# Last-key scores of each head moved into the head's own half of the array

## The chip, the cores and the metric

The kernel runs on one core of one Trainium2 chip. The core has five engines with instruction queues of their own: TensorE (PE, with its weight loads shown as PEld), VectorE (DVE), ScalarE (ACT), GpSimd (POOL) and SyncE (SP). In this kernel SP issues nearly all transfers. Each engine takes its instructions in the order of the program and waits on semaphores. The metric is the device time of one execution in microseconds (us). Before the change it was 1731.4, 1735.86 and 1735.88 us in three runs, median 1735.86.

## The reference

Attention that keeps only the 32 largest scores of each query, followed by a two-layer perceptron with an exact Gelu:

```python
# q, k, v: (8, 8, 576, 64): batch, heads, sequence, head dimension
scores = scale * np.matmul(q, k.transpose(0, 1, 3, 2))
kth = np.partition(scores, -32, axis=-1)[..., -32:-31]
scores = np.where(scores >= kth, scores, -1000000000.0)
scores = scores - np.max(scores, axis=-1, keepdims=True)
attn = np.exp(scores)
attn = attn / (np.sum(attn, axis=-1, keepdims=True) + 1e-09)
x = np.matmul(attn, v)            # then (B,H,S,D) -> (4608, 512)
h = x @ w_in                      # (512, 2048)
g = 0.5 * h * (1.0 + erf(h / sqrt(2)))
return g @ w_out                  # (2048, 512)
```

## The kernel before

Two heads make a pair: the head dimension is 64, so a pair fills the 128 rows of the array, head e in rows 64e to 64e+63. The sequence of 576 is four tiles of 128 queries and a tail of 64. An item of work is one tile of 128 queries for one pair (128 such items), or the tail queries of two pairs (16 items), 144 in all. All products are f32, and an f32 product is carried out as two passes over the array, each with its own weight load: the profile counts passes.

Per item, `scores(i)` makes the scores of 128 queries against 576 keys for both heads, `top_k(i)` finds the 32nd largest value by four rounds of eight maxima on VectorE (lines 324 and 327), `softmax` is four activations on ACT (363, 364), `normalise` is on POOL (375), `transposes` turns the probabilities over on TensorE (392, 409) with copies on ACT, and `attend` multiplies by v (440, 450). The two products of the perceptron (489 and 525) are cut into pieces, and `mlp` puts seven or eight pieces into each step, between the other work of TensorE.

`scores`, the function of the change, uses two tiles of PSUM for an item. `s_ps` has two banks, one for each head, and takes the scores of the 512 main keys; there is one buffer of it. `t_ps` is one bank out of the two of the tag "tp", which transposes, attend's outputs and transpose_qk share, and takes the scores of the 64 last keys of both heads. In `qk`, which `transpose_qk` makes for each pair, columns 0 to 639 are queries, columns 640 to 767 the last keys (block diagonal: head 0's 64 keys in rows 0 to 63 and columns 640 to 703, head 1's in the rest, zeros elsewhere), and columns 768 to 1279 the main keys. Because of those zeros one product over all 128 rows gives the tails of both heads (line 281). The main keys are four products over 64 rows, 256 keys each, in the order head 0, head 1, head 0, head 1 (line 285). Two activations of ACT then scale and evict `s_ps` (289) and `t_ps` (290) to SBUF.

The order is written out by hand and nothing is rescheduled. In step n of the main loop TensorE is given scores of item n+2, attend of n-3, pieces of the perceptron, transposes of n-2 and, at set steps, the transposes of q and k of a coming pair (transpose_qk, line 249). VectorE is given top_k of item n. ACT's order in the step is the eviction of the scores, the copy of attend's output, half or all of the softmax of n-1, the copies of the transposes, Gelus and copies of y as the pieces come up, and in the first steps the conversion of the weights. SP's queue holds, in the same order, the loads of q and k for the pair after next (eight issues of lines 94 and 97, put there by the last piece of transpose_qk), the loads of v (four issues for each pair), the loads of the weights (lines 152 and 161, in the first 17 steps, each waiting for VectorE's or POOL's last use of its staging buffer), and the stores of the output (line 514, each waiting for the ACT copy of y at line 531). No instruction of the score products stands on SP.

Of the kernel before, what the change touches and what calls it, by code (L numbers as in the profile page):

```python
# [14 lines left out]
def kernel(  # L15
# [19 lines left out]
    nc = tc.nc  # L35
# [5 lines left out]
    B, H, S, D = q.shape  # L41
    P = 128
# [5 lines left out]
    SM = NM * P  # L48
    TL = S - SM
# [185 lines left out]
    KT = SM + 2 * P  # L235
# [31 lines left out]
    def spread(t, step, n):  # L267

        return bass.AP(tensor=t.tensor, offset=t.offset, ap=[list(t.ap[0]), [step, 2], [1, n]])

    def scores(i):
        if i >= N:
            return
        pair, t = items[i]
        S_of[i] = s = work.tile([P, 2 * S], f32, tag="s", bufs=5, name="s")
        s_ps = ps.tile([P, 2, 512], f32, tag="s", bufs=1, name="s_ps")
        t_ps = ps.tile([P, 512], f32, tag="tp", name="t_ps")
        if t < NM:
            qk = qk_of[pair]
            lhsT = qk[:, t * P : (t + 1) * P]  # L280
            nc.tensor.matmul(t_ps[:, 0:P], lhsT=lhsT, rhs=qk[:, SM + P : KT], start=True, stop=True)  # L281
            for c in range(2):
                for e in range(2):
                    rows = slice(e * D, (e + 1) * D)
                    nc.tensor.matmul(  # L285
                        s_ps[:, e, c * 256 : (c + 1) * 256], lhsT=lhsT[rows, :],
                        rhs=qk[rows, KT + c * 256 : KT + (c + 1) * 256], start=True, stop=True,
                    )
            nc.scalar.activation(spread(s, S + TL, SM), s_ps, func=AF.Copy, scale=scale)  # L289
            nc.scalar.activation(s[:, SM : S + TL], t_ps[:, 0:P], func=AF.Copy, scale=scale)  # L290
        else:
            for r in range(2):
                qk = qk_of[pair + r]
                lhsT = qk[:, SM : SM + P]
                nc.tensor.matmul(s_ps[:, r, :], lhsT=lhsT, rhs=qk[:, KT:], start=True, stop=True)  # L295
                for e in range(2):
                    nc.tensor.matmul(  # L297
                        t_ps[:, r * TL : (r + 1) * TL], lhsT=lhsT,
                        rhs=qk[:, SM + P + e * TL : SM + P + (e + 1) * TL],
                        start=(e == 0), stop=(e == 1),  # L300
                    )
            s2 = s.rearrange("p (r n) -> p r n", r=2)
            nc.scalar.activation(s2[:, :, 0:SM], s_ps, func=AF.Copy, scale=scale)
            nc.scalar.activation(
                s2[:, :, SM:S], t_ps[:, 0:P].rearrange("p (r n) -> p r n", r=2),
                func=AF.Copy, scale=scale,
            )
# [270 lines left out]
    for pair in range(2):  # L578
        for piece in transpose_qk(pair, pair == 0):
            piece()  # L580
        if pair == 0:
            scores(0)
            scores(1)
# [8 lines left out]
    for n in range(ahead):  # L592

        left[0] = 7 if n < START + 2 * NP else 8
        weights_add(unit_in(n))
        scores(n + 2)
        product = attend(n - 3)
        late = n > START
# [71 lines left out]
```

## Time and profile before

| | |
|---|---|
| profiled execution | 1733.63 us |
| its span | 1731.9 us |
| mean granted TensorE clock | 0.974 |
| TensorE busy | 1632.1 us, 94% of the span |
| VectorE busy | 1428.2 us, 82% |
| ACT busy | 1191.1 us, 69% |
| POOL busy | 664.0 us, 38% |
| tail products (line 281) | 256 passes, 52.9 us |
| main score products (line 285) | 1024 passes, 153.7 us |
| SP transfers issued | 448 |

A line of the timeline gives start, length, engine, source line, operation, and out<-in with its shapes; "xN" means N instructions merged, and the brackets give the engine's idle time before it and what ended it. "SPq" is a transfer being issued on SP; its length is the time for which SP is held by the issue, not that of the transfer. The recorded end of a matmul is modelled, so that the next one can start before it. A line of the windows gives a stretch, its length, the busy time of each engine with the number of its instructions, the granted clock of TensorE and the load on DMA. Busy shares over the whole span are means over stages that have different limits.

### The profile page before, as it was taken

The numbers are of one execution on the slowest core, as the hardware profiler recorded it, in microseconds if no ns is written. First come the engines' busy times: TensorE is split into PE (matmuls) and PEld (weight loads), VectorE is DVE, ScalarE is ACT, GpSimd is POOL, SyncE is SP. The second block draws the span as 40 slices with busy tenths as digits, with TensorE's granted clock in tenths as the row PEclk, the third lists the DMA queues.
The fourth block names the chain that finished last, engine by engine and source line by source line (L and its number), as shares of the span: only waits on it lengthen the run. The fifth ranks groups of instructions, "written<-read, shape, count | busy, mean of one in ns | idle before, by whom it ended". The sixth has DMA issues, their size and how long they took to land.

```text
span 1731.9 us, 24265 instructions
## 1 busy us (share of the span) xinstructions
PE 1632.1 (94%) x8416; PEld 1115.4 (64%) x8416; DVE 1428.2 (82%) x3042; ACT 1191.1 (69%) x2147; POOL 664.0 (38%) x764
## 2 busy tenths in 40 slices
PE   5558999999999999999999999999999999999999
PEld 3335667766666667666666667676666666766665
DVE  7998888988799887997989878898889987899900
ACT  6877767777677767777767666776767766777730
POOL 3677733333333333332333323333333332333310
PEclk8679999999999999999999999999999999999999
DMA  5422310011100111002100011001110010000000
GB/s 155 132 98 91 86 41 1 13 27 28 41 7 13 28 34 34 1 17 45 28 27 1 27 41 41 1 13 27 28 47 1 13 28 14 20 1 13 7 13 13
DMA packets 126716, 56.10 MB, mean 32 GB/s; under 512 B 117889, under 2 KB 117889, under 8 KB 126593
## 3 DMA queue, kind: packets, MB, share of 16 engines
q1 hardware_dynamic: 125056, 52.16, 11.3%
q0 software_dynamic: 320, 2.10, 0.3%
q8 instruction: 67, 1.10, 0.3%
q14 instruction: 57, 0.46, 0.1%
q10 hardware_dynamic: 1216, 0.30, 0.1%
HBM read 45.08 MB, written 9.44 MB: 31 GB/s over the span
## 4 chain that ended last, share of the span: by engine, by line
PE 84%; ACT 5%; POOL 0%; issue 0%; ACTq 0%; POOLq 0%
PE y_ps L525 27%; PE h_ps L489 27%; PE o L440 8%; PE s_ps L285 7%; PE tp L409 7%; PE o L450 2%; PE t_ps L281 1%; PE s_ps L295 1%; PE tp_qk L249 1%; ACT L364 1%; ACT s L364 1%; ACT s L363 1%; PE t_ps L297 1%; PE tp_t L392 1%; POOL s L375 0%; ACT L500 0%
## 5 line engine op out<-in xcount | busy, mean ns | idle before, releaser
L324 DVE MAX8 top<-rest 128x8 f32<-128x576 f32 x864 | 610.3, 749 | 0.0
L489 PE MATMUL h_ps<-xT,w_in_sb 128*128 128x256 f32 (+1 forms) x2560 | 562.9, 364 | 4.3 <-ACT g L500 4.3
L525 PE MATMUL y_ps<-w_out_sb,g 128*128 128x512 f32 x1152 | 545.7, 598 | 0.0
L375 POOL TENSOR_SCALAR s<-s,rden 128x576 f32<-128x576 f32 x288 | 494.3, 1725 | 0.8 <-issue 0.4
L489 PEld LDWEIGHTS h_ps<-xT,w_in_sb 128*128 128x128 f32 x2560 | 432.5, 193 | 67.1 <-issue 15.8
L327 DVE MATCH_REPLACE8 rest<-top,rest 128x576 f32<-128x576 f32 x576 | 423.9, 745 | 0.0
L356 POOL TENSOR_SCALAR den<-den 128x2 f32<-128x2 f32 x144 | 32.1, 223 | 902.1 <-ACT s L364 901.2
L525 PEld LDWEIGHTS y_ps<-w_out_sb,g 128*128 128x128 f32 x1152 | 196.3, 190 | 166.9 <-issue 166.6
L289 ACT ACTIVATE s<-s_ps 128x1024 f32<-128x1024 f32 x128 | 131.6, 1028 | 188.3 <-PE s_ps L285 188.3
L364 ACT ACTIVATE s<-s,bias 128x576 f32<-128x576 f32 x288 | 223.3, 775 | 12.8
L363 ACT ACTIVATE s<-s,neg 128x576 f32<-128x576 f32 x288 | 223.7, 777 | 1.2 <-POOL neg L339 0.7
L416 ACT COPY pt<-tp 128x512 f32<-128x512 f32 x256 | 147.6, 577 | 108.3 <-PE tp L409 107.8
L409 PEld LDWEIGHTS tp<-ident,s 128*128 128x128 f32 x1152 | 148.5, 146 | 113.1 <-issue 59.8
L327 DVE MATCH_REPLACE8 rest<-top,s 128x576 f32<-128x576 f32 x288 | 211.9, 744 | 0.0
L324 DVE MAX8 top<-s 128x8 f32<-128x576 f32 x288 | 202.0, 744 | 5.1 <-ACT s L290 5.1
L409 PE MATMUL tp<-ident,s 128*128 128x128 f32 x1152 | 180.9, 283 | 23.4 <-ACT qk L253 12.8
L350 DVE RECIPROCAL rden<-den 128x2 f32<-128x2 f32 x144 | 23.4, 162 | 213.4 <-POOL den L356 213.4
L285 PE MATMUL s_ps<-qk 64*128 64x256 f32 x1024 | 153.7, 421 | 3.5 <-ACT s L289 3.5
L440 PE MATMUL o<-pt,raw_v 128*64 128x256 f32 x1280 | 153.5, 386 | 2.1 <-ACT pt L416 2.1
L440 PEld LDWEIGHTS o<-pt,raw_v 128*64 128x64 f32 x1280 | 86.8, 138 | 61.1 <-issue 16.1
L285 PEld LDWEIGHTS s_ps<-qk 64*128 64x128 f32 x1024 | 92.6, 195 | 26.8 <-ACT s L289 4.0
L500 ACT ACTIVATE g<-h_ps 128x512 f32<-128x512 f32 x144 | 78.6, 594 | 37.8 <-PE h_ps L489 37.1
(65 smaller groups left out, 1149.8 us busy)
## 6 DMA issues: line engine op xcount, KB each, us to landing
raw_q<-in_q_dram SPq DMA_DIRECT2D x64, 128.0 KB, 2.3
raw_v<-in_v_dram SPq DMA_DIRECT2D x64, 128.0 KB, 2.4
out_dram<-y SPq DMA_DIRECT2D x32, 256.0 KB, 2.2
raw_k<-in_k_dram SPq DMA_DIRECT2D x62, 128.0 KB, 2.4
w_out_sb<-in_moe_w_in_dram SPq DMA_DIRECT2D x12, 511.8 KB, 4.9
w_out_sb<-in_moe_w_out_dram SPq DMA_DIRECT2D x10, 511.8 KB, 3.9
w_out_sb<-in_moe_w_in_dram POOLq DMA_DIRECT2D x4, 511.8 KB, 7.7
words<-in_moe_w_out_dram SPq DMA_DIRECT2D x4, 511.8 KB, 5.1
```

The source lines that it names most:

```text
L285: nc.tensor.matmul(s_ps[:, e, c * 256 : (c + 1) * 256], lhsT=lhsT[rows, :], rhs=qk[rows, KT + c * 256 : KT + (c + 1) * 256], start=True, s ...
L289: nc.scalar.activation(spread(s, S + TL, SM), s_ps, func=AF.Copy, scale=scale)
L324: nc.vector.max(st["top"][:, e, 8 * r : 8 * r + 8], cur[e])
L327: nc.vector.match_replace(rest[:, e], st["top"][:, e, 8 * r : 8 * r + 8], cur[e], LOWEST)
L363: nc.scalar.activation(s, s, func=AF.Prelu, bias=st["neg"][:, e, 1:2], scale=1.0, alpha=STEEP)
L364: nc.scalar.activation(s, s, func=AF.Exp, bias=st["bias"][:, e : e + 1], scale=1.0, accum_out=st["den"][:, e : e + 1],)
L375: nc.gpsimd.tensor_scalar(s, s, st["rden"][:, e : e + 1], None, op0=ALU.mult)
L409: nc.tensor.transpose(tp[:, j * P : (j + 1) * P], s[:, first + j * P : first + (j + 1) * P], ident)
L416: nc.scalar.copy(out=dst, in_=tp.rearrange("p (j n) -> p j n", j=NM))
L440: nc.tensor.matmul(o[e * D : (e + 1) * D, 0:n], lhsT=vt[:, j, e, :], rhs=pt[:, e * NM + j if j < NM else 2 * NM, :], start=(j == 0), stop= ...
L489: nc.tensor.matmul(h_tile(u)[:, i, :], lhsT=w_in_sb[:, ko, f * P : (f + 1) * P], rhs=xT[:, ko, c0 : c0 + n], start=(ko == 0), stop=(ko == ...
L525: nc.tensor.matmul(y_of[sub], lhsT=g_of[u][:, i, sub * P : (sub + 1) * P], rhs=w_out_sb[:, f, :], start=(f == 0), stop=(f == FT - 1),)
```

## The change

The one tail product over 128 rows becomes two products over 64 rows, each with 64 columns and each in its own head's half of the array. Head 0's comes first of the six products of the item, head 1's last. Between them stand the four main products, now in the order head 1, head 0, head 1, head 0. Both tails still write the one bank `t_ps`, in separate columns, from two different halves of the array rows. To keep them apart in time a no-op is put on SP: it waits for the first tail product, and the last tail product waits for it. The evictions and the items of tail queries stay as they are. The order of all other instructions on every engine is unchanged; SP's queue has 128 no-ops more, each in the place where its item's scores stand in the program.

```diff
             lhsT = qk[:, t * P : (t + 1) * P]
-            nc.tensor.matmul(t_ps[:, 0:P], lhsT=lhsT, rhs=qk[:, SM + P : KT], start=True, stop=True)
-            for c in range(2):
-                for e in range(2):
-                    rows = slice(e * D, (e + 1) * D)
-                    nc.tensor.matmul(
-                        s_ps[:, e, c * 256 : (c + 1) * 256], lhsT=lhsT[rows, :],
-                        rhs=qk[rows, KT + c * 256 : KT + (c + 1) * 256], start=True, stop=True,
-                    )
+            tails = [
+                (e, t_ps[:, e * TL : (e + 1) * TL], SM + P + e * TL, TL) for e in range(2)
+            ]
+            mains = [
+                (e, s_ps[:, e, c * 256 : (c + 1) * 256], KT + c * 256, 256)
+                for c in range(2) for e in (1, 0)
+            ]
+            made_by = []
+            for e, dst, at, n in tails[:1] + mains + tails[1:]:
+                rows = slice(e * D, (e + 1) * D)
+                made_by.append(nc.tensor.matmul(
+                    dst, lhsT=lhsT[rows, :], rhs=qk[rows, at : at + n], start=True, stop=True
+                ))
+                if len(made_by) == 1:
+                    between = nc.sync.nop(nofuse=True)
+
+            for a, b in ((between, made_by[0]), (made_by[-1], between)):
+                tc.add_manual_dep(
+                    a.ins, b.ins.name,
+                    mybir.DependencyInfo(mybir.DependencyClass.Sync, mybir.DependencyReason.DATA),
+                    reason="two row tiles, one bank",
+                )
             nc.scalar.activation(spread(s, S + TL, SM), s_ps, func=AF.Copy, scale=scale)
             nc.scalar.activation(s[:, SM : S + TL], t_ps[:, 0:P], func=AF.Copy, scale=scale)
```

## The prediction

> **What bounds the kernel now.** I read the page first, then busy time by stage, then narrow stretches of the timeline around the score products, on TensorE and on SyncE's (SP's) queue.
>
> ```profile
> span 1731.9 us, 24265 instructions
> PE 1632.1 (94%) x8416; PEld 1115.4 (64%) x8416; DVE 1428.2 (82%) x3042; ACT 1191.1 (69%) x2147; POOL 664.0 (38%) x764
> ...
> PE 84%; ACT 5%; POOL 0%; issue 0%; ACTq 0%; POOLq 0%
> ```
>
> ```profile
> 13.90:130.00 116.10, 63.33 (x325) 43.42 (x326) 116.10 (x236) 94.19 (x154) 71.88 (x58) 0.72 0.39 115
> 130.00:240.00 110.00, 98.28 (x506) 68.13 (x505) 94.49 (x192) 78.82 (x136) 76.36 (x58) 0.97 0.24 71
> 240.00:1731.90 1491.90, 1464.19 (x7566) 999.62 (x7564) 1216.50 (x2614) 1015.03 (x1855) 511.20 (x628) 0.99 0.08 21
> ```
>
> The columns are stretch, length, then busy time of PE, PEld, DVE, ACT and POOL, granted clock, DMA. From 13.9 to 130 us VectorE is busy without a gap (116.10 of 116.10); there TensorE has room. From 240 us on TensorE is busy 1464.19 of 1491.90, so only 27.7 us of its idle time could absorb anything: a wait put on TensorE there is paid nearly in full. The sum below is made against the profiled execution, 1733.6 us; the median of the three runs is 2.2 us above it.
>
> **The products themselves.** One score tile, and then an item tail, whose pairs of 64-column products run as four passes (an f32 product is two passes):
>
> ```profile
> 436.37 1.03 PE L489 MATMUL h_ps<-xT,w_in_sb 128*128 128x256 f32 x4
> ...
> 437.24 0.38 PE L281 MATMUL t_ps<-qk 128*128 128x128 f32 x2
> ...
> 437.55 1.14 PE L285 MATMUL s_ps<-qk 64*128 64x256 f32 x8
> ...
> 438.62 2.84 PE L525 MATMUL y_ps<-w_out_sb,g 128*128 128x512 f32 x6
> ```
>
> ```profile
> 200.07 0.55 PE L297 MATMUL t_ps<-qk 128*128 128x64 f32 x4
> 200.56 2.38 PE L440 MATMUL o<-pt,raw_v 128*64 128x256 f32 x20
> ```
>
> From the start of L281 to the start of the next product is 1.38 us, in nearly all the 128 tiles after start-up: 0.31 for the two tail passes (0.11 each and about 0.1 to drain before the array goes over to halves), 1.07 for the eight main passes. Two halves work side by side: eight passes of 256 columns at 0.214 (L525's 512 columns take 0.43) would be 1.71 one after the other; four rounds are 0.86, and 0.2 is the first weight load and the drain out of halves.
>
> Removed: 128 x 2 full passes, 0.22 us a tile. Added: two 64-column passes at the head of half 0, two at the end of half 1. Are they cheaper for being short? L297 says no: four 64-column passes take 0.49 us with the drain, 0.11 each, as long as L281's with 128 columns, since each needs a load of 128 weight columns. So half 0 takes 0.22 + 0.86, which stands where the removed 0.22 stood; half 1's pair ends inside half 0's mains; both drains stay. Net per tile 0. Bounds: if a short pass took no longer than its columns, -0.11 a tile (-14 us); if the halves went on in step, one round for each unequal pair, six rounds for the former four and the 0.22: +0.21 a tile (+27 us). I take 0, which L297 is nearest to.
>
> **The wait through SP.** The last tail product waits for a no-op on SP, the no-op for the first tail product. When SP is free this is over in time: the first tail is done some 0.4 us into the tile, the last is due 1.0 us after the point where L281 starts today. But SP issues in program order, and each issue holds it. In the tile above:
>
> ```profile
> 436.57 0.37 SPq L94 DMA_DIRECT2D raw_q<-in_q_dram  x1
> ...
> 437.55 0.58 SPq L94 DMA_DIRECT2D raw_q<-in_q_dram  x1
> ...
> 440.56 0.51 SPq L97 DMA_DIRECT2D raw_k<-in_k_dram  x1
> ```
>
> Eight issues of transpose_qk's loads stand ahead of the no-op; the last ends at 441.07, the tail is due at 438.25. With 0.2 us for the no-op and two semaphores (an estimate; ACT's copy to SP's issue below is 0.03, a last main pass to L289 0.48) TensorE stops for 3.0 us, with everything queued behind the tail: the y_ps products, transposes, all else. ACT's t_ps eviction waits with it, and ACT's softmax behind that. The other kind:
>
> ```profile
> 247.69 0.38 PE L281 MATMUL t_ps<-qk 128*128 128x128 f32 x2
> ...
> 248.93 1.08 ACT L531 COPY y<-y_ps 128x512 f32<-128x512 f32 x2
> 249.06 2.50 PE L450 MATMUL o<-ptt,raw_v 128*128 128x128 f32 x20
> ...
> 249.54 0.85 SPq L514 DMA_DIRECT2D out_dram<-y  x2
> ```
>
> A pair of stores waits for the y copies, which ACT does behind two Gelus; SP is free at 250.39, the tail was due at 248.70: 1.9 us.
>
> The changed program's order puts a known issue last before each no-op, so I set its end against the tile's L281 start + 1.01, for all 128 tiles. From the fourteenth tile (132.7 us) on, 35 of 115 are late: 18 behind stores (1.9 to 2.2 us, sum 35.3), 15 behind load bursts (0.4 to 3.7, sum 30.5), 2 behind weight loads (0.2 and 5.1). **Sum 71.0 us.** The other 80 lose nothing. Bounds: hops of 0.05 to 0.4 give 66 to 78; the slack of 27.7 can take off that much at most, though its waits lie elsewhere than these stops. DMAs queued behind a no-op wait for later TensorE or ACT work anyway: 0. More no-ops on an SP that is idle cost 0; what hides them is SP's idle time, and where that is gone the cost is the 71.
>
> **Start-up.** The first no-op stands behind 20 issues of SP.
>
> ```profile
> 13.88 1.42 DVE L324 MAX8 top<-s 128x8 f32<-128x576 f32 x2 [5.14 <-ACT s L290]
> ```
>
> ```profile
> 17.55 0.51 SPq L97 DMA_DIRECT2D raw_k<-in_k_dram  x1
> ```
>
> VectorE starts on the first tile at 13.88, as its t_ps eviction ends; now that comes after 18.06 + 0.2 + passes and eviction 0.9 = 19.2: +5.3. VectorE bounds the stretch to 130 us, so this stays. In the next steps SP has 8 loads (4.6), 4 loads of v (2.4) and weights (0.8) ahead of no-ops, and ACT must evict t_ps before the softmax (3.3) on which VectorE's reciprocal waits one tile (9.65) later. Where both bursts fall into one step, 7.8 + 3.3 exceeds it by 1.5; I count four such steps, 6. Bounds 0 and 10 for these. Later tiles to 130 us wait some 5 us behind weight loads, into gaps of 4 to 7 us in which TensorE waits for POOL now: 0. **Sum 11**, bounds 5 and 15.
>
> **The clock.** What a stop does to TensorE's clock is in two stretches around today's longest late gap (2.13 us, ACT's copy of qk), and in one like it cut by a window's edge:
>
> ```profile
> 359.34:362.75 3.41, 1.74 (x10) 1.10 (x9) 3.41 (x9) 3.27 (x6) 0.00 (x0) 1.00 0.00 0
> ...
> 451.49:454.91 3.42, 1.29 (x8) 0.88 (x7) 3.42 (x8) 2.79 (x5) 0.00 (x0) 1.00 0.29 62
> 454.91:458.32 3.41, 3.41 (x11) 2.77 (x10) 1.20 (x4) 2.71 (x5) 0.99 (x4) 0.50 0.00 0
> ```
>
> A stretch of 3.4 us with TensorE busy 1.29 is followed by one at half clock, one with 1.74 is not. Half clock for 3.41 us costs 1.7 at most. Of a stop, about 0.4 is the tail's own loads and drain, so stops of 3.0 and more (8) leave gaps over 2.5, of which some two thirds fall so that a stretch falls short; stops of 1.9 to 2.2 (20) leave 1.5 to 1.8, at the edge: I take one in ten. 5.5 + 2 = 7.5 at 1.6: **12 us**, bounds 0 and 43 (all 28 with the longest at two).
>
> The Trainium skill's "TensorE: Matmul & The Clock Gate" (Part 1: The HAM clock gate) has the clock fall after a whole idle window, and advises gaps under about 3.4 us. By that one stop alone, 5.1, would pay, and the sum would be some 10 lower, by estimate near 1819. This trace's 2.13 us gap did pay.
>
> **Sum:** 1733.6 + 0 + 71.0 + 11 + 12 = 1827.6; with the median standing a little higher, **1829 us**.
>
> **Rivals.**
> 1. Clock falls after nearly every stop: 12 becomes 43, 1859. For it: 2.13 was enough. Against: 1.67 idle in one stretch was not.
> 2. Halves in step: +27, 1855. For: main passes start in pairs in today's program. Against: their lengths are equal, so that shows nothing of unequal ones, and nothing makes one half wait for the other.
> 3. Stops partly absorbed: the 27.7 of idle time goes into them and the clock holds: 1733.6 + 71 - 27.7 + 11 = 1788; with short passes (-14), 1774.
> 4. Faster: the no-op is over before it matters, because SP's queue does not hold it behind its issues, and the short passes take their columns only: 1733.6 - 14 = 1720. It decides if SP is done 1.0 us into the tile; SP's own records (441.07 against 438.25) speak against it.
> 5. No change: no-op free as in 4, tails costing what L297 says: 1734; the same evidence against it.
>
> **How the numbers follow.** Chances: forecast 0.62 (own range 1805 to 1850), rival 1 0.13, rival 2 0.10, rival 3 0.11, rival 4 0.02, rival 5 0.02. Leaving out half of rival 3 below and the upper part of rivals 1 and 2 gives 1785 to 1862. Measurement tells 0.3% (5 us) from no change: faster 0.02, same 0.02, slower 0.96.
>
> **What would show it.** Right: tail products on TensorE (or their weight loads) idle some 70 us in total with SP as releaser, about 35 waits of 1 to 5 us late in the run; 1.38 us from tile to next product wherever SP is free; first MAX8 near 19 us; about 7 more half-clock stretches after 130 us; VectorE, ACT and POOL with unchanged busy time. Wrong if the stops are not there or are much shorter than SP's record says, if tiles without a stop take 1.27 or 1.6 us, or if the stops shift other work so that later waits vanish.

## The result and the profile after

The changed kernel takes 1828.37 us (median of five runs, 1824.57 to 1834.1), the kernel before 1733.78 us (five runs). The ratio is 1.0554, with a 95% interval of 1.053 to 1.0579: slower by 5.5%. The forecast was 1829 us. The profiled execution has a span of 1822.8 us, 90.9 more than before.

The page of the changed kernel, its first lines, the chain and three groups (the score products now have line 293, the no-op 297, the eviction of `t_ps` 306, `top_k`'s maxima 340):

```profile
span 1822.8 us, 24906 instructions
PE 1676.2 (92%) x8672; PEld 1136.8 (62%) x8672; DVE 1428.8 (78%) x3042; ACT 1192.3 (65%) x2147; POOL 662.0 (36%) x764
...
PE 75%; ACT 8%; SPq 3%; issue 2%; POOL 0%; ACTq 0%; POOLq 0%
...
L340 DVE MAX8 top<-s 128x8 f32<-128x576 f32 x288 | 202.0, 744 | 10.0 <-ACT s L306 10.0
L293 PEld LDWEIGHTS t_ps<-qk 64*128 64x128 f32 x512 | 86.8, 199 | 172.0 <-SPq L297 99.2
L293 PE MATMUL t_ps<-qk 64*128 64x64 f32 x512 | 107.4, 295 | 82.6 <-SPq L297 77.5
```

VectorE, ACT and POOL do what they did before, to within 2 us of busy time. SP's queue has entered the chain that ended last, and the tail products now stand idle for SP's no-op: 77.5 us of TensorE.

The tile that the prediction showed (437.24 us before, the last tail due at 438.25) now begins at 469.79. Its stretch of the timeline:

```profile
469.79 0.32 PE L293 MATMUL t_ps<-qk 64*128 64x64 f32 x1
...
470.06 1.08 PE L293 MATMUL s_ps<-qk 64*128 64x256 f32 x7
...
473.01 0.51 SPq L97 DMA_DIRECT2D raw_k<-in_k_dram  x1
473.64 0.43 PE L293 MATMUL t_ps<-qk 64*128 64x64 f32 x2 [2.50 <-SPq L297]
474.00 2.85 PE L541 MATMUL y_ps<-w_out_sb,g 128*128 128x512 f32 x3
474.11 0.28 ACT L306 ACTIVATE s<-t_ps 128x128 f32<-128x128 f32 x1 [1.84 <-PE t_ps L293]
```

The first tail and the mains are done by 471.1. The second tail waits for the last of eight load issues, which ends at 473.52, and starts 0.12 us later. The y_ps products behind it start at 474.00 and not at 471.07, where a tile without a stop would have let them: 2.9 us. A tile without a stop looks like this:

```profile
337.95 0.32 PE L293 MATMUL t_ps<-qk 64*128 64x64 f32 x1
337.96 0.48 PE L293 MATMUL s_ps<-qk 64*128 64x256 f32 x1
338.12 0.27 PE L293 MATMUL t_ps<-qk 64*128 64x64 f32 x1
338.23 0.86 PE L293 MATMUL s_ps<-qk 64*128 64x256 f32 x6
338.93 0.22 PE L293 MATMUL t_ps<-qk 64*128 64x64 f32 x1
338.93 0.38 PE L293 MATMUL s_ps<-qk 64*128 64x256 f32 x1
338.99 0.27 PE L293 MATMUL t_ps<-qk 64*128 64x64 f32 x1
339.24 1.95 PE L456 MATMUL o<-pt,raw_v 128*64 128x256 f32 x16
```

The two short passes of half 0 run at its head beside a main pass of half 1, those of half 1 at its end beside a main pass of half 0. The tile lasts 1.28 us, and the drain of 0.1 that used to stand between the tail and the mains now stands ahead of it: 1.38 again.

The windows around the stop at 473 show the clock (the last columns are granted clock, DMA share, GB/s):

```profile
470.71:474.12 3.41, 0.91 (x8) 0.45 (x5) 3.41 (x8) 1.03 (x2) 1.10 (x1) 1.00 0.55 123
474.12:477.53 3.41, 3.41 (x5) 1.35 (x6) 3.41 (x8) 1.79 (x4) 0.00 (x0) 0.50 0.07 15
477.53:480.95 3.42, 3.42 (x15) 1.84 (x14) 0.12 (x1) 1.23 (x3) 0.00 (x0) 1.00 0.00 0
```

A stretch with TensorE busy 0.91 us of 3.41 is followed by one at half clock, with five passes of y_ps in it or at its edges, where full clock has room for eight. After 190 us the clock of every trace here changes only at the edges of such stretches of 3.41 us, the grid of the clock; one stretch at half clock, or two in a row, is called a spell below.

Setting the 128 score tiles of the two traces beside each other, tile by tile, gives the whole difference:

| part | predicted us | in the traces us |
|---|---|---|
| start-up, until the sixteenth tile (it begins at 159.8 us before, at 176.9 after; 0.1 of that is the drain) | 11 | 17.0 |
| stops from there on | 71.0 in 35 | 65.3 in 34 |
| spells at half clock after 190 us, about 1.7 each | 12 (7.5 more) | about 12 (12 against 5; one of the 12 is two stretches long) |
| what is left over: waits of before that vanish behind a stop | 0 | about -3 |
| sum | 94 | 91 of 90.9 |

### The profile page after: what moved, and what is told of

Read it like the earlier page. It is cut to its first block, busy times and chain, and to the rows that moved or that the text cites. A ratio compares the mean times of both kernels' runs of the same rounds, so it can differ in the third digit from the quotient of the medians.

```text
span 1822.8 us, 24906 instructions
## 1 busy us (share of the span) xinstructions
PE 1676.2 (92%) x8672; PEld 1136.8 (62%) x8672; DVE 1428.8 (78%) x3042; ACT 1192.3 (65%) x2147; POOL 662.0 (36%) x764
## 4 chain that ended last, share of the span: by engine, by line
PE 75%; ACT 8%; SPq 3%; issue 2%; POOL 0%; ACTq 0%; POOLq 0%
PE h_ps L505 25%; PE y_ps L541 24%; PE o L456 8%; PE tp L425 6%; PE s_ps L293 4%; PE o L466 2%; PE t_ps L293 2%; PE tp_qk L249 1%; PE s_ps L311 1%; ACT s L379 1%; ACT g L516 1%; SPq L94 1%; SPq L97 1%; ACT s L380 1%; ACT L380 1%
## 5 line engine op out<-in xcount | busy, mean ns | idle before, releaser
L541 PE MATMUL y_ps<-w_out_sb,g 128*128 128x512 f32 x1152 | 555.0, 606 | 0.0
L293 PEld LDWEIGHTS t_ps<-qk 64*128 64x128 f32 x512 | 86.8, 199 | 172.0 <-SPq L297 99.2
L293 PE MATMUL s_ps<-qk 64*128 64x256 f32 x1024 | 186.1, 423 | 0.0
L293 PE MATMUL t_ps<-qk 64*128 64x64 f32 x512 | 107.4, 295 | 82.6 <-SPq L297 77.5
L456 PE MATMUL o<-pt,raw_v 128*64 128x256 f32 x1280 | 164.5, 407 | 2.1 <-ACT pt L432 2.1
L293 PEld LDWEIGHTS s_ps<-qk 64*128 64x128 f32 x1024 | 121.8, 201 | 6.6
```

The source lines that it names most:

```text
L293: made_by.append(nc.tensor.matmul(dst, lhsT=lhsT[rows, :], rhs=qk[rows, at : at + n], start=True, stop=True))
L456: nc.tensor.matmul(o[e * D : (e + 1) * D, 0:n], lhsT=vt[:, j, e, :], rhs=pt[:, e * NM + j if j < NM else 2 * NM, :], start=(j == 0), stop= ...
L541: nc.tensor.matmul(y_of[sub], lhsT=g_of[u][:, i, sub * P : (sub + 1) * P], rhs=w_out_sb[:, f, :], start=(f == 0), stop=(f == FT - 1),)
```

## The experiments

**The wait alone.** The kernel before, with only the no-op added, so that the last main product waits for the tail product over SP:

```diff
-            nc.tensor.matmul(t_ps[:, 0:P], lhsT=lhsT, rhs=qk[:, SM + P : KT], start=True, stop=True)
+            made_by = [
+                nc.tensor.matmul(t_ps[:, 0:P], lhsT=lhsT, rhs=qk[:, SM + P : KT], start=True, stop=True)
+            ]
+            between = nc.sync.nop(nofuse=True)
...
+            for a, b in ((between, made_by[0]), (made_by[-1], between)):
+                tc.add_manual_dep(
...
```

> The products of before (one full tail product, then the mains over halves), with only the no-op on SP added: it waits for the tail product, and the last main product waits for it. Theory (the stops behind SP's issues are the whole loss): the last main is due some 0.27 us earlier in its tile than the last tail of the changed kernel, so each of about 36 late stops after 130 us is longer by that: 1828 + 10 = 1838 us, within 1825 to 1850; some 36 waits on SP after 130 us. Rival (the split into halves costs the time, the wait is hidden): 1734 us.

Measured: 1863.12 us, ratio 1.0759 (1.074 to 1.0777). The direction and the place are the theory's, the size is not: 25 us more than expected. The rival, no change, is out. All waits of its trace for SP's no-op:

```profile
PEld s_ps L288 <- SPq L284: 98.8, 43, 6.9
PE s_ps L288 <- SPq L284: 77.1, 37, 6.2
```

and VectorE's waits up to 140 us, of this kernel and then of the changed one:

```profile
DVE rden L359 <- POOL den L365: 17.6, 5, 7.2
DVE top L333 <- ACT s L299: 11.5, 1, 11.5
```

```profile
DVE top L340 <- ACT s L306: 10.0, 1, 10.0
DVE rden L366 <- POOL den L372: 9.4, 4, 5.0
```

By the tiles' starts, start-up costs 27.8 us and not 17.0, and 34 later stops cost 77.2 and not 65.3. The middle one of them is longer by 0.26, as expected (0.27); a few behind load bursts are longer by 0.8 or more, among them some whose held product itself ran at half clock. TensorE's idle gaps are nearly all as long as in the changed kernel (2.5 us behind a load burst, 1.4 behind a store in both), but 19 spells at half clock follow after 200 us and not 12, four of them two stretches long and not one; between the stops the trace loses some 15 us more. I put this down to where the gaps fall on the clock's grid; no run varies that alone.

For start-up, what I had left out is what the held product is for. In the changed kernel a stop holds the eviction of `t_ps`, 0.28 us of ACT; here it holds that of `s_ps`, 1.02 us, behind which ACT's softmax waits too. The longer waits of VectorE for the reciprocals (17.6 us against 9.4) fit this, but no run shows it by itself.

**The halves alone.** Head 0's tail at the head of half 0, the changed order of the mains, no no-op and no second tail:

```diff
-            for e, dst, at, n in tails[:1] + mains + tails[1:]:
+            for e, dst, at, n in tails[:1] + mains:
...
```

> Head 0's tail product at the head of half 0 and the mains in the changed order, with no no-op and no wait. Head 1's tail product is left out; the eviction reads head 0's tail scores twice, at the same size. Half 1 is the shorter half, so half 0 still sets the tile. Theory: 1.28 us from the first tail pass to the next product plus 0.1 of drain moved ahead of it, as before: 1734 us, within 0.3%. Rival (halves cost time by themselves): 1760 us or more.

Measured: 1730.74 us, ratio 0.9993 (0.9979 to 1.0007). No change. Its tiles last 1.28 us, as those of the changed kernel without a stop do. So the split into halves neither costs nor gains, and the gain that a shorter product might have had is not there. That the omitted tail would be free is seen in the changed kernel's own tiles, which have it.

**All transfers behind the no-op.** The changed kernel; `load`, `load_weights` and `store` put themselves on a list, which is emptied right behind the scores of the step:

```diff
+        if holding[0]:
+            pending.append(lambda: store(tok, y))
+            return
...
         scores(n + 2)
+        flush()
```

> The changed kernel, with all of SP's transfers after the first loads held back and issued behind the no-op of the next score tile instead of ahead of it. Theory: SP is free at each no-op, no stop is left, nor start-up delay or half clock from them: 1734 us, within 0.5%, and fewer than 5 waits on SP of over 0.5 us. Rival (the trip over SP costs time in every tile): 0.2 us or more for each of 128 tiles, 1760 us or more.

Measured: 1730.3 us, ratio 0.9991 (0.9975 to 1.0008). The same 128 no-ops and the same wait in each tile, and nothing is left of the loss. All waits of its trace for SP's no-op:

```profile
PEld t_ps L307 <- SPq L311: 1.9, 2, 1.6
PE t_ps L307 <- SPq L311: 0.8, 1, 0.8
```

This is the clearest of the runs: the round trip itself costs nothing here, and what costs is the place of the no-op in SP's queue.

**The first 13 items alone** have the changed products and the wait:

```diff
+            if i < 13:
...
+            else:
...
```

> The changed products and the wait in the first 13 items only, the products of before in the rest. Theory: start-up alone. The prediction had 11 us for it; the shift between the two traces by the fifteenth item is 16.8, so 1734 + 17 = 1751 us, with some 1.5 less if later waits of TensorE take in a part. Rival (the early delay is taken up later, when TensorE is the bound): 1736 us.

Measured: 1750.53 us, ratio 1.0103 (1.0078 to 1.0128), which is 18 us (13 to 22). In its one trace the shift is 20.7 us by the sixteenth tile and still 20.6 at the last: the delay made while VectorE is the bound was not given back in the TensorE-bound stage behind it. The rival of this run, that it is taken up, is out.

**Only the loads, or only the stores, behind the no-op:**

The list of the run with all transfers now takes only the loads, or only the stores. The part for `load`; `load_weights` and `store` have the like:

```diff
         if pair >= n_pairs:
             return
+        if holding[0]:
+            pending.append(lambda: load(n, pair, queue))
+            return
...
```

> The changed kernel with the loads of q, k, v and of the weights issued behind the next no-op, the stores still ahead of it. Theory: start-up and the stops behind loads (31.7 us by the trace of the changed kernel) go; 18 stops behind stores stay, 33.6 us, with gaps of some 1.4 us that take the clock down two or three times: 1733 + 34 + 4 = 1771 us. Rival (the stops are TensorE's own wait for the round trip, whatever SP is doing): no change, 1828 us.

Measured: 1768.98 us, ratio 1.0213 (1.0196 to 1.0231). TensorE's waits for the no-op after 150 us, 18 of 1.4 us on average, are those behind the stores:

```profile
PE t_ps L307 <- SPq L311: 25.7, 18, 1.7
```

There are four spells at half clock after 190 us, one fewer than before the change. Three of them stand right behind stops (gaps of 1.34, 1.36 and 1.66 us), as expected. But four of the five of before are gone, although the gaps of 2.1 us that caused them are all still there: they come later and no longer take so much out of one stretch of the clock's grid. So the 4 us that I had for the clock were paid and given back.

> The changed kernel with only the stores issued behind the next no-op. Theory: start-up stays (16.8 us less some 3 absorbed after it), 16 stops behind loads stay (31.7 us), with gaps of 2 to 2.6 us that take the clock down about six times at 1.7 us: 1733 + 14 + 32 + 10 = 1789 us.

Measured: 1797.96 us, ratio 1.0377 (1.0359 to 1.0396), 9 more than expected. Its tiles show a shift of 18.5 us by the sixteenth one, 16 stops behind loads, and 13 spells at half clock after 190 us, four of them two stretches long: 17 stretches, twelve more than before, where I had six.

```profile
PE t_ps L301 <- SPq L305: 25.6, 11, 4.5
```

The two savings, 59.4 and 30.4 us, make up 90 of the 95 us lost. Each run keeps only one kind of stop, so the loss is made of two separate kinds of traffic ahead of the same no-op.

**A version without the wait that gains.** The halves alone gain nothing: a pass of 64 columns took 0.11 us, as long as one of 128 (L297 and L281 in the prediction), which I put down to its weight load; no run separates the two. (The pair at the end of half 1 above starts 0.06 us apart, but beside a main pass that takes longer anyway.) A pass of 320 columns is far above that (0.27 us from one to the next in the rows below). So in 52 items each head has one product of 256 keys and one of 320, its tail among them, and no separate tail product. The two products of 320 columns go to two banks of the shared pair, so no wait is needed:

```diff
+        if i in merged:
...
+                    if c == 0:
+                        dst, at, n = s_ps[:, e, 0:256], KT + (64 if e == 0 else 0), 4
+                    else:
+                        dst, at, n = half[e][:, 0:320], SM + P + e * TL, 5
+                    nc.tensor.matmul(
+                        dst.rearrange("p (a b) -> p a b", b=64), lhsT=lhsT,
+                        rhs=keys(at, n, rows), start=True, stop=True,
+                    )
```

`keys` takes n blocks of 64 keys, 128 columns apart.

> The kernel before; in 52 of the 128 items (those whose step has neither attend's product nor transposes of q and k behind the scores) there is no tail product: each head has one main product of 256 keys and one of 320 with its tail, in its own half, the latter of each head in a bank of its own of the shared pair, so that no wait is needed; keys are taken in another order of 64-key blocks and put back by the evictions. Theory: a tile costs two rounds of 0.214 and two of 0.268 and the two changes of mode, 1.26 instead of 1.38: 52 x 0.116 = 6 us less, 1727 us (ratio 0.9965), if ACT frees the two banks before the transposes need them. Rival (both shared banks are held too long, TensorE waits for ACT in these steps): 1735 us or more.

Measured: 1725.04 us, ratio 0.996 (0.9946 to 0.9973), as expected. In this first version the eviction puts the blocks of head 0's second product one place off, so that its scores stand under other keys; the work is the same.

In the second version head 0's tail block is evicted by itself:

```diff
+            nc.scalar.activation(
+                place(0, 4), t_ps[:, 64:320].rearrange("p (a b) -> p a b", b=64),
+                func=AF.Copy, scale=scale,
+            )
+            nc.scalar.activation(s[:, SM : SM + TL], t_ps[:, 0:64], func=AF.Copy, scale=scale)
```

> As merged_odd, with head 0's tail block evicted by an activation of its own, which puts it in its place (one more small activation in each of the 52 items, some 0.2 us of ACT each, beside TensorE's work). Theory: as before this, ratio 0.996, 1726 us.

Measured: 1724.12 us, ratio 0.9948 (0.9934 to 0.9962). This is the whole computation, faster than the kernel before by 0.5% and than the changed one by 104 us. Not all of it is the shorter tile: in its trace some 5 of the 8 us come a good 0.1 at a time from merged tiles, and some 3 from having three spells at half clock after 190 us where the trace of before has five.

The third takes in the items whose step has attend's product:

```diff
-        if items[i][1] < NM and not done_before and i - 2 not in prep_at:
+        if items[i][1] < NM and i - 2 not in prep_at:
```

> As merged_52, in 108 of the 128 items: also in those whose step has attend's product right behind the scores. Theory: those 56 tiles gain 0.116 us each as well, but attend's output must now wait until ACT has evicted one of the two shared banks, some 1.5 us behind the last pass: 1726 + 56 x 1.2 = 1790 us. Rival (ACT is quick enough): 1719 us.

Measured: 1787.24 us, ratio 1.0308 (1.0289 to 1.0327). A merged tile and the next product, and then the waits, of this kernel:

```profile
340.27 0.70 PE L300 MATMUL s_ps<-qk 64*128 64x256 f32 x4
340.81 0.43 PE L300 MATMUL t_ps<-qk 64*128 64x320 f32 x1
340.82 0.43 PE L300 MATMUL u_ps<-qk 64*128 64x320 f32 x1
341.08 0.43 PE L300 MATMUL t_ps<-qk 64*128 64x320 f32 x1
341.09 0.43 PE L300 MATMUL u_ps<-qk 64*128 64x320 f32 x1
341.45 2.84 PE L566 MATMUL y_ps<-w_out_sb,g 128*128 128x512 f32 x6
```

```profile
ACT xT L486 <- PE o L481: 121.6, 62, 4.3
...
PEld o L481 <- ACT s L314: 72.6, 40, 5.0
```

The merged tile is 1.18 us and 0.1 of drain ahead of it, against 1.38. But with both shared banks held, attend's product stands until ACT has evicted one: its weight loads wait 72.6 us for the evictions, 40 times. The version pays only where other work of TensorE lies between the scores and the next user of those banks.

## Why the prediction was right

The time was right to 1 us, which is closer than its terms were.

*The products, net 0.* Right. L297's rows carried it: 1.281 + 0.1 in the trace, and a ratio of 0.9993 with the halves alone. The rivals with halves in step (+27) and with short passes at the time of their columns (-14) are both out.

*The stops, 71.0 us in 35.* The mechanism was right: with the transfers out of the way (all of them issued behind the no-op) nothing of the loss is left. 34 of them came, 65.3 us. The estimated hop of 0.2 us was too long: the tail starts 0.12 after SP's last issue, which takes some 3 us off the sum. Two stops that I had at 1.2 and 1.5 came at 0.3. One of them rested on a single issue that took 1.54 us in the trace of before and 0.51 in that of after, so that a duration from one execution was taken for a rule:

```profile
371.58 1.54 SPq L97 DMA_DIRECT2D raw_k<-in_k_dram  x1
```

```profile
398.14 0.51 SPq L97 DMA_DIRECT2D raw_k<-in_k_dram  x1
```

*Start-up, 11 us.* Under by 6: 17.0 in the trace of the changed kernel. The same early items gave 18.5 in the trace with only the stores moved and 20.7 in that of the first 13 items alone, and 18 by the times of the latter, so the term moves by some 2 us from one execution to the next. The first maxima came at 18.19 and not at 19.2 (+4.3 for +5.3), since the burst ahead of the first no-op began 0.7 us earlier in that execution and ended 1.0 earlier. The terms that were too small are the later ones. VectorE waited 9.4 us for the reciprocals of four early tiles, where I had 6 in all. And it waited again, beyond 140 us, where I had nothing; first the trace of before, then that of after:

```profile
148.83 0.17 DVE L350 RECIPROCAL rden<-den 128x2 f32<-128x2 f32 x1 [6.39 <-POOL den L356]
```

```profile
146.26 0.17 DVE L366 RECIPROCAL rden<-den 128x2 f32<-128x2 f32 x1 [0.52 <-POOL den L372]
165.85 0.17 DVE L366 RECIPROCAL rden<-den 128x2 f32<-128x2 f32 x1 [8.57 <-POOL den L372]
```

These are 2.7 us more, and with them the shift of VectorE's maxima is the 17.0 of the tiles.

*Later tiles up to 130 us, 0.* Nearly right: two of the four early waits for reciprocals, 0.35 and 0.52 us, came from them, and a third of 0.52 at 146 us.

*The clock, 12 us.* Right in the sum, 12 spells against 5, but with luck in the parts. Of the six stops of 2.9 us and more after 190 us four were followed by half clock (I had 5.5 of 8), of the 21 of about 2 us four (I had 2 of 20). One spell came behind a gap of 2.1 us that the trace of before has too, without a fall, and three of the five of before came again. Reading the term from the 2.13 us gap, and not from the rule of a whole idle window in the Trainium skill's "TensorE: Matmul & The Clock Gate" (Part 1: The HAM clock gate), was the right choice: the spells behind stops followed gaps of 1.4 to 2.6 us, all shorter than such a window, and by the rule the forecast would have been near 1819, by the prediction's estimate. Rival 1, a fall after nearly every stop, is out too: it was 8 of 27.

*Nothing absorbed.* Some 3 us were. Behind the stop of the sixteenth tile (5.3 us) and the tile after it, waits of TensorE that the trace of before has (160 to 236 us) are smaller or gone in that of after (176 to 257 us):

```profile
PE tp L409 <- ACT pt L393: 1.9, 2, 1.1
PE tp_t L397 <- POOL s L375: 1.2, 1, 1.2
...
PE tp_t L392 <- POOL s L375: 1.0, 1, 1.0
PE h_ps L489 <- ACT g L500: 0.5, 1, 0.5
```

```profile
PE tp L425 <- ACT pt L409: 0.8, 1, 0.8
```

Rival 3 had set the whole 27.7 us of idle time against the stops; what was taken up are waits that come soon after a stop.

So the start-up was 6 short, the stops 6 long and the absorbed waits 3 unseen; they nearly cancel. The mechanism carried the forecast to within a few microseconds of each term; that the total came out within 1 us, less than the 10 us over which the five runs spread, is luck.

## What to carry to other kernels

An instruction that only passes a semaphore on is as late as the queue it stands in. Before a wait is led over an engine, read when that engine finishes the last thing ahead of it, tile by tile, against the time at which the waiting engine would come to it; moving the transfers behind the no-ops took a loss of 95 us to nothing.

A shorter product is not always a cheaper one: here a pass of 64 columns took as long as one of 128. Join it to a longer one with the same weights rather than splitting it off, if the banks that this needs come free in time. And when an engine is stopped, ask what the held result releases: the same wait on the main product cost 37 us more than on the tail (132 against 95), 11 of them in start-up, where the held eviction is the likely cause.

## What the runs showed of the hardware

The two halves of the array ran unequal passes side by side: in the tile at 337.95 us the two short passes of half 0 (337.95 and 338.12) run beside the first main pass of half 1 (337.96). The tile lasts 1.28 us, where halves that went on in step would have needed 1.49, by the prediction's sum for that rival.

TensorE's clock fell after partly idle stretches. Over the eleven traces I set TensorE's busy time, by its matmul records, in each 3.41 us stretch of the clock's grid after 190 us against the clock of the next stretch. Where a stretch at full clock had under 1.5 us of busy time, the next was at half clock in every case (57 of 57); between 1.5 and 2.1 us in 22 of 76; above 2.1 us in none of 4835. Ten of the 90 stretches at half clock were followed by a second one, with 1.6 to 3.4 us of busy time in the first. A half-clock stretch mostly showed in the shift of the tiles as 1.6 to 1.7 us. Within each trace all changes of the clock after 190 us lie on one grid of 3.41 us, to 0.01 us. So the same kind of gap, 2.1 us behind ACT's copy of qk, six of them in each of the three traces, was followed by half clock five times before the change, three times after it and once with the loads behind the no-op.
